# A cross network on one Trainium2 core: the state is kept as a factor c, and the last sums move to TensorE

## The chip, the cores and the metric

The kernel runs on one core of a Trainium2 chip. A core has five engines with queues of their own: TensorE (PE, matmuls; PEld is its weight load), VectorE (DVE), ScalarE (ACT), GpSimd (POOL) and SyncE (SP), which here only issues DMA. SBUF is the working memory with 128 partitions; PSUM holds what TensorE accumulates. The metric is the device time of one execution in microseconds, as the median of several runs. Before the change it is 131.3 us (three runs, 131.0 to 131.58).

## The reference

```python
B, F, D, L = 4096, 26, 16, 6          # Din = 416
x = x0
for l in range(6):
    x = x0 * (x @ ws[l] + bs[l]) + x
return x
```

All data are bf16. x0 is 4096 x 416, ws is 6 x 416 x 416. Every layer multiplies elementwise by the same x0 and adds the old x. So every x is x0 times some factor c: c starts at 1 and gains x @ ws[l] + bs[l] in each layer.

## The kernel before

The state is held transposed: the features lie on the partitions and the 4096 rows of the batch along the free axis. The 416 features are three full blocks of 128 (index m or k, tiles `XM`) and a remainder of 32. The remainders of four groups of 512 rows are packed on the 128 partitions of `XR`. The batch is cut in two halves (s = 0, 1) of 2048 rows, each of four groups (g) of 512.

Layer 0 (`first_layer`, L208) and layers 1 to 4 (the loop from L282) compute the transposed product. A tile is a pair (s, m): 48 matmuls of 512 columns (L181) and four for the remainder rows (L187) fill two PSUM tiles (`pts`, h = 0, 1) of 128 x 1024. PSUM holds four such tiles in all (pool `psum`, 4 buffers), and they are handed on in a ring. `finish` calls `ew_main` for each h: ScalarE moves the tile out of PSUM and adds the bias (L165), VectorE multiplies by x0 (L166) and adds the old state (L169). The tiles of a layer are taken in pairs: (0,0), (0,1), then the remainder of both halves (`rem_pair`), then (0,2), (1,0), then (1,1), (1,2). The input of each layer and its output alternate between `XM[1]` and `XM[2]`.

Layer 5 (from L315) is computed with the batch rows on the partitions, so that its result can be stored directly: 32 blocks of 128 rows x 416 columns, eight "quads" (`quads`) of four blocks. For each block TensorE runs three matmuls of 416 columns (L327), one for the remainder (L333) and one for the bias (L336). Then `ew` (L347): ScalarE casts out of PSUM (L354), VectorE multiplies by rows of x0 (`X0rows`, L355), adds rows of the layer-4 state (`XLrows`, L344), and the block is stored. The addition of one block is pinned behind the multiplication of the next (`pending`, `close_sum`). Nine groups are handled as pairs, the other 14 blocks singly; the final store is issued from ScalarE's queue, the others from SyncE's.

`XLrows` is the layer-4 state turned back to rows by DMA: `xl_dmat` (L204) issues one transpose of 128 x 2048 per tile (s, m) when that tile's state is ready, and `rem_pair` issues one small transpose per half into `scrR`. `xl_rem` (L276) lets ScalarE copy `scrR` into the last 32 columns of `XLrows`. It is pinned (`keep_in_program_order`): the copy for half 0 stands in ScalarE's queue in front of the four evacuations of tiles (1,1) and (1,2), the copy for half 1 behind them.

Each engine works through its own queue in order. A scheduler places the instructions of one program on the queues and adds the semaphore waits; instructions marked `keep_in_program_order` are not moved.

Of the kernel before, what the change touches and what calls it, by code (L numbers as in the profile page):

```python
# [9 lines left out]
ACT = mybir.ActivationFunctionType  # L10
ALU = mybir.AluOpType
# [5 lines left out]
def kernel(  # L17
# [7 lines left out]
    nc = tc.nc  # L25
# [23 lines left out]
    dz = const.tile([P, 2], FP32)  # L49
    warm = const.tile([P, CW], BF16)  # L50
    ones = const.tile([P, P], BF16)
    WM = const.tile([P, L, NK, D], BF16)
    WR = const.tile([P, L, D], BF16)
    WD = const.tile([P, L, NG, R], BF16)
    bsb = const.tile([L, D], BF16)
    bLr = const.tile([P, D], BF16)
    bM = const.tile([P, NK, L], FP32)
    bR = const.tile([P, L], FP32)
    X0rows = big.tile([P, NBT, D], BF16)
    XLrows = big.tile([P, NBT, D], BF16)  # L60
    scrR = [big.tile([P, 4, P], BF16, name=f"scrR{s}") for s in range(NS)]
    xrem = big.tile([P, 16, R], BF16)
    xrig = big.tile([P, NS, 4, P], BF16)
    XRd = big.tile([P, NS * CW], BF16)
    XM = [big.tile([P, NK, B], BF16, name=f"XM{i}") for i in range(3)]
    XR = [big.tile([P, NS * CW], BF16, name=f"XR{i}") for i in range(3)]

    def col0(s, g):
        return SW * s + CW * g
# [76 lines left out]
    def bias_setup():  # L146
        pb = psum.tile([P, 4, 8], BF16, tag="ps", name="pb")
        for m in range(NK):
            nc.tensor.transpose(pb[:, m, 0:L], bsb[0:L, 128 * m:128 * m + 128], ident[0:L, 0:L])
        for g in range(NG):  # L150
            nc.tensor.transpose(pb[32 * g:32 * g + 32, 3, 0:L], bsb[0:L, NK * P:D], ident[0:L, 0:L], tile_position=(0, 32 * g))  # L151
        nc.vector.tensor_copy(bM[:], pb[:, 0:NK, 0:L])  # L152
        nc.vector.tensor_copy(bR[:], pb[:, 3, 0:L])

    def x0_rem(s, tpr):
        for i in range(4):
# [2 lines left out]
            to = XR[0] if dst == src else XRd  # L159
            nc.vector.tensor_copy(to[dst, CW * s:CW * s + CW], tpr[src])  # L160

    def ew_main(l, s, m, h, pt, cur, nxt, pin=False):
        c0 = col0(s, 2 * h)
        t = tpool.tile([P, 2 * CW], BF16, name="t")
        nc.scalar.activation(t[:], pt[:].rearrange("p a b -> p (a b)"), ACT.Identity, bias=bM[:, m, l:l + 1], scale=1.0)  # L165
        prod = nc.vector.tensor_tensor(out=t[:], in0=t[:], in1=XM[0][:, m, c0:c0 + 2 * CW], op=ALU.mult)  # L166
        if pin:
            tc.keep_in_program_order(prod)
        nc.vector.tensor_tensor(out=nxt[:, m, c0:c0 + 2 * CW], in0=t[:], in1=cur[:, m, c0:c0 + 2 * CW], op=ALU.add)  # L169

    def ew_rem(l, s, pr, curR, nxtR):
        tr = tpool.tile([P, 2 * CW], BF16, name="t")
        nc.scalar.activation(tr[:, 0:CW], pr, ACT.Identity, bias=bR[:, l:l + 1], scale=1.0)  # L173
        nc.vector.tensor_tensor(out=tr[:, 0:CW], in0=tr[:, 0:CW], in1=XR[0][:, CW * s:CW * s + CW], op=ALU.mult)  # L174
        nc.vector.tensor_tensor(out=nxtR[:, CW * s:CW * s + CW], in0=tr[:, 0:CW], in1=curR[:, CW * s:CW * s + CW], op=ALU.add)  # L175

    def mm_full(l, s, m, g, pts, cur, first, last):
        c0 = col0(s, g)
        for k in range(NK):
            for q in range(4):  # L180
                nc.tensor.matmul(pts[g // 2][32 * q:32 * q + 32, g % 2, :], lhsT=WM[:, l, k, 128 * m + 32 * q:128 * m + 32 * q + 32],  # L181
                                 rhs=cur[:, k, c0:c0 + CW], start=(first and k == 0), stop=(last and k == NK - 1),
                                 tile_position=(0, 32 * q))

    def mm_row(l, s, m, pts, curR, first, last):
# [5 lines left out]
    def mm_rem(l, s, pr, cur, curR):  # L191
        for g in range(NG):
            nc.tensor.matmul(pr[32 * g:32 * g + 32, :], lhsT=WD[:, l, g, :], rhs=curR[:, CW * s:CW * s + CW],  # L193
                             start=True, stop=False, tile_position=(0, 32 * g))
        for k in range(NK):
            for g in range(NG):
                c0 = col0(s, g)
                nc.tensor.matmul(pr[32 * g:32 * g + 32, :], lhsT=WM[:, l, k, NK * P:D], rhs=cur[:, k, c0:c0 + CW],  # L198
                      start=False, stop=(k == NK - 1), tile_position=(0, 32 * g))

    def new_pts():
        return [psum.tile([P, 2, CW], FP32, tag="ps", name=f"pt{h}") for h in range(2)]

    def xl_dmat(s, k, nxt):  # L204
        nc.sync.dma_start_transpose(out=XLrows[:, 16 * s:16 * s + 16, 128 * k:128 * k + 128],
                                    in_=nxt[:, k, SW * s:SW * s + SW])

    def first_layer(s):  # L208
        cur, curR, nxt, nxtR = XM[0], XR[0], XM[1], XR[1]

        def full(pt, m, h, gl, after_row):
            c0 = col0(s, 2 * h + gl)
            for k in range(NK):
                nc.tensor.matmul(pt[:, gl, :], lhsT=WM[:, 0, k, 128 * m:128 * m + 128], rhs=cur[:, k, c0:c0 + CW],  # L214
                                 start=(k == 0 and not after_row), stop=(k == NK - 1 and after_row))

        def row(pt, m, h, opens):
# [25 lines left out]
        row(pa[2], 2, 0, False)  # L243
        row(pa[1], 1, 0, False)
        for m in range(NK):
            ew_main(0, s, m, 0, pa[m], cur, nxt)
        for m in range(NK):
            if m:
                pb.append(ph(m))
# [6 lines left out]
        if s == 0:  # L256
            x0_rem(1, pr[:, 1, :].bitcast(BF16)[:, 0:CW])
        for m in range(NK):
            ew_main(0, s, m, 1, pb[m], cur, nxt, pin=(s == 0))
        ew_rem(0, s, pr[:, 0, :], curR, nxtR)  # L260

    bias_setup()
    pe_filler(1, CW)
    for s in range(NS):
        first_layer(s)

    def rem_pair(l, cur, curR, nxtR, feeds_last):
        pr2 = psum.tile([P, 2, CW], FP32, tag="ps", name="pr2")
        for s in range(NS):
            mm_rem(l, s, pr2[:, s, :], cur, curR)  # L270
        for s in range(NS):
            ew_rem(l, s, pr2[:, s, :], curR, nxtR)
            if feeds_last:
                nc.sync.dma_start_transpose(out=scrR[s][:], in_=nxtR[:, CW * s:CW * s + CW])

    def xl_rem(s):  # L276
        tc.keep_in_program_order(
            nc.scalar.copy(XLrows[:, 16 * s:16 * s + 16, NK * P:D].rearrange("p (g i) r -> p i g r", g=NG),
                           scrR[s][:].rearrange("p i (g r) -> p i g r", g=NG)))

    cur, curR = XM[1], XR[1]
    for l in range(1, LL):  # L282
        nxt, nxtR = XM[1 + (l % 2)], XR[1 + (l % 2)]
        feeds_last = (l == LL - 1)
        tiles = [(s, m) for s in range(NS) for m in range(NK)]
        pts = {}

        def finish(t):
            s, m = t
            for h in range(2):  # L290
                ew_main(l, s, m, h, pts[t][h], cur, nxt)
            if feeds_last:
                xl_dmat(s, m, nxt)

        for n in range(0, len(tiles), 2):
            ta, tb = tiles[n], tiles[n + 1]
            pts[ta] = new_pts()
            for g in range(NG):
                mm_full(l, ta[0], ta[1], g, pts[ta], cur, True, False)
            mm_row(l, ta[0], ta[1], pts[ta], curR, False, True)  # L300
            pts[tb] = new_pts()
            mm_row(l, tb[0], tb[1], pts[tb], curR, True, False)
            if feeds_last and n == 4:
                xl_rem(0)
            finish(ta)
            for g in range(NG):
                mm_full(l, tb[0], tb[1], g, pts[tb], cur, False, True)
            finish(tb)
            if n == 0:
                rem_pair(l, cur, curR, nxtR, feeds_last)  # L310
        if feeds_last:
            xl_rem(1)
        cur, curR = nxt, nxtR
# [3 lines left out]
    NQ = len(quads)  # L317
    KD = NK * P

    def q_cols(q, g):  # L320
        s, i = quads[q]
        c = col0(s, g) + 128 * i
        return slice(c, c + 128)

    def mm_q_full(q, g, py, closes):
        for k in range(NK):
            nc.tensor.matmul(py[:, 0:D], lhsT=cur[:, k, q_cols(q, g)], rhs=WM[:, l, k, :],  # L327
                             start=((not closes) and k == 0), stop=(closes and k == NK - 1))

    def mm_q_rem(q, py, done):  # L330
# [7 lines left out]

    pending = []

    def close_sum():
        while pending:
            o, t, xl, dst, eng = pending.pop()
            tc.keep_in_program_order(nc.vector.tensor_tensor(out=o, in0=t, in1=xl, op=ALU.add))  # L344
            eng.dma_start(dst, o)

    def ew(q, g0, n, src, eng):  # L347
        s, i = quads[q]
        b0 = 16 * s + 4 * g0 + i
        b = slice(b0, b0 + 4 * (n - 1) + 1, 4)  # L350
        t = tpool.tile([P, 2 * CW], BF16, name="t")
        o = opool.tile([P, 2, D], BF16, name="o")
        tv = t[:, 0:n * D].rearrange("p (a d) -> p a d", a=n)
        nc.scalar.copy(tv, src)  # L354
        tc.keep_in_program_order(nc.vector.tensor_tensor(out=tv, in0=tv, in1=X0rows[:, b, :], op=ALU.mult))  # L355
        close_sum()
        pending.append((o[:, 0:n, :], tv, XLrows[:, b, :], out_v[:, b, :], eng))

    PAIRS = [(0, 0), (0, 1), (1, 0), (1, 1), (2, 0), (2, 1), (3, 0), (3, 1)]
    TURNS = [(0, 0), (0, 1), (1, 0), (2, 0), (3, 0), (1, 1), (2, 1), (3, 1)]  # L360
# [2 lines left out]
    for q, at, done in rounds:  # L363
# [12 lines left out]
        for u in range(done, 8):  # L376
# [2 lines left out]
                close(u, 1)  # L379
            elif u % 2:  # L380
                close(u - 1, 2)
    close_sum()


# [28 lines left out]
```

## Time and profile before

| what | value |
|---|---|
| median of three runs | 131.3 us (131.0 to 131.58) |
| profiled execution, first to last instruction (span) | 128.9 us |
| profiled execution, whole time | not recorded; span and median differ by 2.4 us |
| mean granted TensorE clock | 0.998 |
| TensorE busy | 123.1 us, 96% of the span |
| VectorE busy | 107.1 us, 83% |
| ScalarE busy | 86.9 us, 67% |
| layer 5 begins on TensorE | 103.78 us |

Times inside the span are counted from its start. A group's row gives the line, the engine, the operation, what it writes and reads, how often, its busy time and the mean time of one. A number in brackets in the timeline is the time that the engine stood idle before the row, and what released it. In SyncE's queue the duration of a row is the time that issuing took, not the time of the transfer.

### The profile page before, as it was taken

The numbers are of one execution on the slowest core, as the hardware profiler recorded it, in microseconds if no ns is written. First come the engines' busy times: TensorE is split into PE (matmuls) and PEld (weight loads), VectorE is DVE, ScalarE is ACT, GpSimd is POOL, SyncE is SP. The second block draws the span as 40 slices with busy tenths as digits, with TensorE's granted clock in tenths as the row PEclk, the third lists the DMA queues.
The fourth block names the chain that finished last, engine by engine and source line by source line (L and its number), as shares of the span: only waits on it lengthen the run. The fifth ranks groups of instructions, "written<-read, shape, count | busy, mean of one in ns | idle before, by whom it ended". The sixth has DMA issues, their size and how long they took to land.

```text
span 128.9 us, 3973 instructions
## 1 busy us (share of the span) xinstructions
PE 123.1 (96%) x1690; PEld 54.9 (43%) x1690; DVE 107.1 (83%) x197; ACT 86.9 (67%) x99; POOL 5.9 (5%) x18
## 2 busy tenths in 40 slices
PE   6999999999999999999999999999999999999960
PEld 2343443354444444444444444444444445445420
DVE  1032979999999898989898989898989899898991
ACT  0426783987848577848668848668847896569670
POOL 4022200600000000000000000000000000000000
PEclk9999999999999999999999999999999999999999
DMA  3999999999990000000000000000297999995754
GB/s 106 237 203 217 170 158 260 247 328 333 336 299 11 5 0 8 0 0 5 0 5 0 5 0 5 0 5 0 42 166 164 123 219 178 187 323 188 231 179 139
DMA packets 42102, 16.37 MB, mean 127 GB/s; under 512 B 30906, under 2 KB 42084, under 8 KB 42084
## 3 DMA queue, kind: packets, MB, share of 16 engines
q1 hardware_dynamic: 39416, 15.56, 54.6%
q10 hardware_dynamic: 2668, 0.56, 2.3%
q8 instruction: 13, 0.21, 0.7%
q14 instruction: 5, 0.04, 0.1%
HBM read 6.15 MB, written 3.41 MB: 74 GB/s over the span
## 4 chain that ended last, share of the span: by engine, by line
PE 80%; DMA 8%; DVE 5%; issue 2%; SPq 1%; ACT 1%; DVEq 0%
PE pt L181 49%; PE ph L214 9%; DMA XM<-in_x_dram 8%; PE py L327 8%; PE pt L187 5%; PE pr L198 5%; DVE t L355 3%; DVE o L344 2%; PE pr L193 2%; SPq L76 1%; PE py L333 1%; PE ph L221 1%; PE py L336 1%; ACT t L354 1%; PE pr L157 0%
## 5 line engine op out<-in xcount | busy, mean ns | idle before, releaser
L181 PE MATMUL pt<-XM,WM 128*32 128x512 bf16 x1152 | 65.2, 379 | 0.0
L165 ACT ACTIVATE t<-pt,bM 128x1024 bf16<-128x1024 f32 x48 | 49.6, 1115 | 18.3 <-PE pt L187 18.3
L166 DVE TENSOR_TENSOR t<-t,XM 128x1024 bf16<-128x1024 bf16 x60 | 41.4, 690 | 5.3 <-ACT t L165 5.3
L169 DVE TENSOR_TENSOR XM<-t,XM 128x1024 bf16<-128x1024 bf16 x60 | 41.8, 696 | 3.4
L181 PEld LDWEIGHTS <-WM 128*32 128x32 bf16 x1152 | 29.7, 97 | 33.8 <-issue 5.1
L354 ACT CAST t<-py 128x416 bf16<-128x416 f32 (+1 forms) x23 | 14.8, 642 | 4.8 <-PE py L327 2.1
L327 PE MATMUL py<-WM,XM 128*128 128x416 bf16 x96 | 17.7, 340 | 0.0
L214 PE MATMUL ph<-XM,WM 128*128 128x512 bf16 x72 | 16.5, 379 | 0.1
L165 ACT ACTIVATE t<-ph,bM 128x1024 bf16<-128x1024 f32 x12 | 12.5, 1114 | 4.4 <-PE ph L221 4.4
L327 PEld LDWEIGHTS <-XM 128*128 128x128 bf16 x96 | 9.0, 98 | 8.5 <-issue 1.4
L355 DVE TENSOR_TENSOR t<-t,X0rows 128x416 bf16<-128x416 bf16 (+1 forms) x23 | 10.4, 454 | 1.2 <-ACT t L354 1.2
L214 PEld LDWEIGHTS <-WM 128*128 128x128 bf16 x72 | 6.8, 98 | 8.6 <-issue 1.3
L344 DVE TENSOR_TENSOR o<-t,XLrows 128x416 bf16<-128x416 bf16 (+1 forms) x23 | 10.3, 451 | 0.0
L173 ACT ACTIVATE t<-pr,bR 128x512 bf16<-128x512 f32 x10 | 6.4, 684 | 2.7 <-PE pr L198 2.1
L198 PE MATMUL pr<-XM,WM 128*32 128x512 bf16 x120 | 8.2, 379 | 0.0
L187 PE MATMUL pt<-XR,WR 32*128 32x512 bf16 x96 | 7.3, 379 | 0.0
L141 PE MATMUL wps<-warm 128*128 128x512 bf16 (+1 forms) x11 | 4.4, 593 | 1.2 <-DVE warm L94 1.2
L175 DVE TENSOR_TENSOR XR<-t,XR 128x512 bf16<-128x512 bf16 x10 | 4.2, 423 | 0.7
L198 PEld LDWEIGHTS <-WM 128*32 128x32 bf16 x120 | 3.2, 97 | 3.1
L106 ACT ACT_TABLE_LOAD x1 | 1.3, 1283 | 4.3 <-DMA WM<-in_ws_dram 4.3
L174 DVE TENSOR_TENSOR t<-t,XR 128x512 bf16<-128x512 bf16 x10 | 4.2, 418 | 0.0
L152 DVE CAST bM<-pb 128x18 f32<-128x18 bf16 x1 | 0.2, 177 | 4.6 <-PE pb L151 4.6
(39 smaller groups left out, 33.6 us busy)
## 6 DMA issues: line engine op xcount, KB each, us to landing
X0rows<-in_x_dram SPq DMA_DIRECT2D x4, 832.0 KB, 11.6
out_dram<-o SPq DMA_DIRECT2D x9, 208.0 KB, 2.4
WM<-in_ws_dram SPq DMA_DIRECT2D x5, 312.0 KB
out_dram<-o SPq DMA_DIRECT2D x13, 104.0 KB, 1.7
WR<-in_ws_dram SPq DMA_DIRECT2D x4, 130.0 KB, 4.1
WM<-in_ws_dram ACTq DMA_DIRECT2D x1, 312.0 KB
XM<-in_x_dram SPq DMA_TRANSPOSE x8, 4.9
xrig<-in_x_dram ACTq DMA_DIRECT2D x4, 32.0 KB, 4.1
```

Of the source, the lines that this page charges most:

```text
L165: nc.scalar.activation(t[:], pt[:].rearrange("p a b -> p (a b)"), ACT.Identity, bias=bM[:, m, l:l + 1], scale=1.0)
L166: prod = nc.vector.tensor_tensor(out=t[:], in0=t[:], in1=XM[0][:, m, c0:c0 + 2 * CW], op=ALU.mult)
L169: nc.vector.tensor_tensor(out=nxt[:, m, c0:c0 + 2 * CW], in0=t[:], in1=cur[:, m, c0:c0 + 2 * CW], op=ALU.add)
L173: nc.scalar.activation(tr[:, 0:CW], pr, ACT.Identity, bias=bR[:, l:l + 1], scale=1.0)
L181: nc.tensor.matmul(pts[g // 2][32 * q:32 * q + 32, g % 2, :], lhsT=WM[:, l, k, 128 * m + 32 * q:128 * m + 32 * q + 32], rhs=cur[:, k, c0:c ...
L187: nc.tensor.matmul(pts[g // 2][:, g % 2, :], lhsT=WR[32 * g:32 * g + 32, l, 128 * m:128 * m + 128], rhs=curR[32 * g:32 * g + 32, CW * s:CW ...
L198: nc.tensor.matmul(pr[32 * g:32 * g + 32, :], lhsT=WM[:, l, k, NK * P:D], rhs=cur[:, k, c0:c0 + CW], start=False, stop=(k == NK - 1), tile ...
L214: nc.tensor.matmul(pt[:, gl, :], lhsT=WM[:, 0, k, 128 * m:128 * m + 128], rhs=cur[:, k, c0:c0 + CW], start=(k == 0 and not after_row), sto ...
L327: nc.tensor.matmul(py[:, 0:D], lhsT=cur[:, k, q_cols(q, g)], rhs=WM[:, l, k, :], start=((not closes) and k == 0), stop=(closes and k == NK ...
L344: tc.keep_in_program_order(nc.vector.tensor_tensor(out=o, in0=t, in1=xl, op=ALU.add))
L354: nc.scalar.copy(tv, src)
L355: tc.keep_in_program_order(nc.vector.tensor_tensor(out=tv, in0=tv, in1=X0rows[:, b, :], op=ALU.mult))
```

## The change

The kernel now keeps the factor c (`CM`, `CR`) beside x. In layer 0 ScalarE writes c directly (the bias of layer 0 has 1 added to it), and VectorE multiplies c by x0 to get x1. In layers 1 to 4 VectorE adds the layer's result into c in place and then multiplies c by x0 to get the next x. `XM[2]` and `XLrows` are gone: x after an odd layer lies in `shared`, one buffer per half, and the same buffer takes the rows of c at the end. So what the DMA turns back to rows is c of layer 4 (`cl_dmat`, `cl_dmat_rem`), and it is written over x2, the input of layer 4.

In layer 5 a block becomes (sum + c) times x0: VectorE adds the rows of c to the cast block, then multiplies by `X0rows` into the output (`close_out`). For the last three blocks of the 32 (`SUM_ON_PE = 3`) TensorE adds the rows of c itself, by a product with the identity into the same PSUM tile; two of these are then cast and multiplied, and the very last is multiplied by VectorE straight out of PSUM, without a cast.

```diff
+    CM = big.tile([P, NK, B], BF16)
+    shared = [big.tile([P, 16, D], BF16, name=f"shared{s}") for s in range(NS)]
-    XLrows = big.tile([P, NBT, D], BF16)
...
+        nc.vector.tensor_scalar_add(bM[:, :, 0:1], bM[:, :, 0:1], 1.0)
+        nc.vector.tensor_scalar_add(bR[:, 0:1], bR[:, 0:1], 1.0)
...
-        t = tpool.tile([P, 2 * CW], BF16, name="t")
-        nc.scalar.activation(t[:], pt[:].rearrange("p a b -> p (a b)"), ACT.Identity, bias=bM[:, m, l:l + 1], scale=1.0)
-        prod = nc.vector.tensor_tensor(out=t[:], in0=t[:], in1=XM[0][:, m, c0:c0 + 2 * CW], op=ALU.mult)
+        c = CM[:, m, c0:c0 + 2 * CW]
+        if l == 0:
+            nc.scalar.activation(c, pt[:].rearrange("p a b -> p (a b)"), ACT.Identity, bias=bM[:, m, 0:1], scale=1.0)
+        else:
+            t = tpool.tile([P, 2 * CW], BF16, name="t")
+            nc.scalar.activation(t[:], pt[:].rearrange("p a b -> p (a b)"), ACT.Identity, bias=bM[:, m, l:l + 1], scale=1.0)
+            nc.vector.tensor_tensor(out=c, in0=c, in1=t[:], op=ALU.add)
+        prod = nc.vector.tensor_tensor(out=nxt(m, s, 2 * h * CW, 2 * CW), in0=c, in1=XM[0][:, m, c0:c0 + 2 * CW], op=ALU.mult)
...
-        nc.vector.tensor_tensor(out=nxt[:, m, c0:c0 + 2 * CW], in0=t[:], in1=cur[:, m, c0:c0 + 2 * CW], op=ALU.add)
...
+    def cl_dmat(s, k):
+        tc.keep_in_program_order(nc.sync.dma_start_transpose(out=shared[s][:, :, 128 * k:128 * k + 128],
+                                                             in_=CM[:, k, SW * s:SW * s + SW]))
...
             finish(ta)
+            if feeds_last and n == 2:
+                cl_dmat(0, 0)
+                cl_dmat(0, 1)
+                cl_dmat_rem(0)
+                cl_dmat_rem(1)
...
             finish(tb)
+            if feeds_last and n == 2:
+                cl_dmat(0, 2)
+            if feeds_last and n == 4:
+                cl_dmat(1, 0)
+                cl_dmat(1, 1)
+                cl_dmat(1, 2)
...
+        if by_pe(q, g):
+            nc.tensor.matmul(py[:, 0:D], lhsT=ident[:], rhs=shared[s][:, 4 * g + i, :], start=False, stop=False)
...
+        if 4 * q + g0 == 4 * NQ - 1:
+            close_out()
+            tc.keep_in_program_order(nc.vector.tensor_tensor(out=o[:, 0:1, :], in0=src, in1=xr, op=ALU.mult))
+            eng.dma_start(dst, o[:, 0:1, :])
+            return
...
-        tc.keep_in_program_order(nc.vector.tensor_tensor(out=tv, in0=tv, in1=X0rows[:, b, :], op=ALU.mult))
-        close_sum()
-        pending.append((o[:, 0:n, :], tv, XLrows[:, b, :], out_v[:, b, :], eng))
+        if not by_pe(q, g0):
+            tc.keep_in_program_order(nc.vector.tensor_tensor(out=tv, in0=tv, in1=shared[s][:, r, :], op=ALU.add))
+        close_out()
+        pending.append((o[:, 0:n, :], tv, xr, dst, eng))
```

## The prediction

> **What bounds the kernel now.** I read the page first (busy shares, chain), then the chain in order of time, then the timeline around the hand-over from layer 4 to layer 5 and at the end, then SyncE's queue alone in short windows, one transpose per answer.
>
> ```profile
> span 128.9 us, 3973 instructions
> PE 123.1 (96%) x1690; PEld 54.9 (43%) x1690; DVE 107.1 (83%) x197; ACT 86.9 (67%) x99; POOL 5.9 (5%) x18
> PE 80%; DMA 8%; DVE 5%; issue 2%; SPq 1%; ACT 1%; DVEq 0%
> ```
>
> TensorE is busy 96% of the span and holds 80% of the chain. In order of time the chain is TensorE without a gap from 12.14 us to 115.78 us. So VectorE's and ScalarE's work costs nothing as long as it keeps ahead; a TensorE that must wait costs its whole wait.
>
> ```profile
> 92.00 2.76 PE L181 MATMUL pt<-XM,WM 128*32 128x512 bf16 x48
> 100.02 0.62 ACT L278 COPY XLrows<-scrR 128x512 bf16<-128x512 bf16 x1 [0.76 <-DMA scrR<-XR]
> 100.97 4.13 ACT L165 ACTIVATE t<-pt,bM 128x1024 bf16<-128x1024 f32 x4 [0.33 <-PE pt L187]
> 105.31 0.34 PE L333 MATMUL py<-WR,XR 32*128 32x416 bf16 x4
> 122.80 1.75 PE L327 MATMUL py<-WM,XM 128*128 128x416 bf16 x9
> 123.00 2.09 ACT L354 CAST t<-py 128x416 bf16<-128x416 f32 x4
> 125.39 0.37 DVE L355 TENSOR_TENSOR t<-t,X0rows 128x416 bf16<-128x416 bf16 x1
> 125.67 0.65 DVE L344 TENSOR_TENSOR o<-t,XLrows 128x416 bf16<-128x416 bf16 x2
> 126.35 0.38 ACTq L345 DMA_DIRECT2D out_dram<-o  x1
> ```
>
> These are start, duration, engine and line, from the timeline (core 0; the rows between are left out of the fence). The first is the last tile of half 0 in layer 4: its matmuls end at 94.76. The second is ScalarE's pinned copy of the remainder columns, which already waits 0.76 for the small transpose. The four activations behind it evacuate tiles (1,1) and (1,2); they end at 105.10, and TensorE takes the last freed buffer at 105.31 to 105.40. The slack is about a quarter of a microsecond. The last five rows are the tail.
>
> ```profile
> 91.63 2.03 SPq L205 DMA_TRANSPOSE XLrows<-XM  x1
> 94.35 3.07 SPq L205 DMA_TRANSPOSE XLrows<-XM  x1
> 97.52 2.53 SPq L274 DMA_TRANSPOSE scrR<-XR  x2
> 102.26 3.67 SPq L205 DMA_TRANSPOSE XLrows<-XM  x1
> scrR<-XR SPq DMA_TRANSPOSE x2, 2.5
> ```
>
> SyncE's queue: issuing one large transpose holds it 1.8 to 3.7 us, a small one 1.2 us, and a small one lands 2.5 us after its issue (last line, from the list of DMA issues): 97.52 + 2.5 = 100.02, exactly where ScalarE's copy starts.
>
> **Part 1, c in place of x (layers 0 to 4).** Layer 0 loses one of two VectorE operations per tile: 12 of 0.69 us and 2 of 0.42 us, 9.1 us. In layers 1 to 4 an add into c and a multiply replace a multiply and an add of the same shapes; x is ready after two operations as before. TensorE runs gapless over all this, so I take 0; a gain would need a TensorE gap that the chain does not show. The two additions of 1 to the biases (nearest rows: small VectorE casts of 0.18 us) fall into the 2.4 us in which VectorE waits for the remainder transposes at 8.6 us; cost 0, at most 0.36 without that cover.
>
> **Part 2, the transposes.** In the new order the rows of c go into the buffer that also holds the layer's input x2, so the first transpose of a half waits for the last matmul that reads x2 of that half. In the built program SyncE waits for exactly that matmul of tile (0,2): issue at 94.8 instead of 91.63. Behind it in SyncE's queue stand (0,1), both small transposes, (0,2), the three of half 1 and the outputs. Two large issues come before the small one. I take them as the same pair lasts before, 2.03 + 3.07, with 0.1 between issues: the small one starts at 100.1. The lower bound is 1.81 twice (the shortest large issue in the queue), giving 98.6; the upper 3.07 + 3.67, giving 101.7. I stay near the middle because the second issue of each pair was long in three pairs out of three (3.07, 3.67, 3.62). With 2.5 to landing: 102.6 (101.1 to 104.2).
>
> ScalarE's copy is pinned in front of the four activations and cannot be passed. It ends at 102.6 + 0.62 = 103.2; the four activations need 4.13 and end at 107.35 (105.85 to 108.95). TensorE needs the last of their buffers at 105.35, so it stops for **2.0 us** (0.5 to 3.6). A first short stop at 103.8, for tile (1,1)'s first buffer, lies inside this.
>
> What is late next: the (0,2) transpose, issued about 102.7, lands within 6.1 us (the median of the large ones), 108.8; VectorE ends layer 4 at 107.65 + 2.0 = 109.6, so the first addition of c is covered by 0.8. Half 1's transposes wait for TensorE at 103.9, before SyncE reaches them; at 2.7 us each (the mean of the six is near that) the last is issued at about 110.7 and lands at 116.8, against a first use at 116.69 + 2.0 = 118.7. VectorE then needs 1.0 us per pair of blocks (two operations started 0.5 apart) where TensorE needs 1.29, so a lag there is made up. Outputs start after 111.6 before; no engine waits for them until the end. Cost 0, up to 1 us if both covers fail.
>
> The rule against this step: the Trainium skill, "DMA: Bandwidth & Descriptors", section "Rules for kernel authors", says to issue a DMA early and wait for it late, so that its fixed cost hides under compute. Its loss, were the fixed cost all that is moved, would be the 3.2 us of later issue less 0.6 of slack, a stop of 2.6 us, and the sum would be +2.0 us instead of mine; the queue's rows give less, because the 0.65 us in which SyncE stands between the first two issues (93.66 to 94.35) goes.
>
> **Part 3, the end.** TensorE gains three matmuls 128x416: 96 such take 17.7 us, 0.184 each, +0.55 us; its last ends 124.55 + 0.55 = 125.10. Removed behind it: the last cast (0.51), one multiply and the additions of the last three blocks. Before, VectorE is the late one: two operations of 0.285 spacing per block, 0.57, against 0.54 of TensorE; it ends at 126.32. After, blocks 25 to 28 take two operations as before and are done by 124.3, block 29's multiply follows its cast, block 30's cast ends at 124.9 and its multiply lets the last one in at 125.2. That one reads f32 from PSUM, which no VectorE row here of this width does. Bounds: 0.37 (the bf16 multiply) and 0.69 (1024 wide); I take 0.51, ScalarE's cast of the same f32 tile. End 125.7, a gain of **0.6 us** (0.4 to 0.8). The output behind it leaves the same queue with the same landing.
>
> The Trainium skill, "VectorE: DVE Perf Modes", section "The TRN2 errata", prices a PSUM source at 120 cycles plus one per f32 element at 0.96 GHz: an estimate of 0.56 us for 416, which would make the gain 0.55.
>
> **Sum.** +2.0 − 0.6 = +1.4 us on a span of 128.9. The profiled execution's whole time is not recorded; span and median leave 2.4 us around it (2.1 to 2.7 for the runs of 131.0 to 131.58), which I keep. 131.3 + 1.4 = **132.7 us**. Ends: 131.3 + 0.5 − 0.8 = 131.0 and 131.3 + 3.6 − 0.4 = 134.5.
>
> **Rivals.**
> 1. The small transpose lands in time, and only the tail is left: faster. It decides if it lands before 105.35 − 4.13 − 0.62 = 100.6, so is issued by 98.1, with two large issues in 3.2 us. For it: some large issues take 1.8 us, and the stop of the transposes' packets that made others long need not come then. Against: no row has 1.6. Time 131.3 − 0.6 = 130.7, and 130.5 with the best tail.
> 2. A partial stop: both large issues short (1.81 to 2.03), the small one lands near 101.3; stop 0.5 to 1.2 us, net −0.1 to +0.6: 131.5. For it: with no wait between them the pair may run at the rate of the fast ones.
> 3. Half 1's rows come late too (upper issue times throughout): VectorE stands at block 16, its backlog holds ScalarE's buffers and TensorE stops a second time, about 1 us more: 133.7 to 134.5. For it: 1.9 us of cover against an issue spread of 1.9 us each. Against: the stop of TensorE moves the need later by the same amount.
> 4. TensorE's clock falls in the stop. The granted clock is 1.00 in every working window, and 0.94 in the 4.4 us after the last matmul: half speed only in the last half microsecond or so of it, hence about 3.9 us after work ended; the stop would have to be twice mine. Cost then: the cold fillers at the start ran 4.45 us, about half of it lost, +2.2 us: 134.9. The Trainium skill, "TensorE: Matmul & The Clock Gate", section "Part 1", puts the fall after one idle window of about 3.4 us; by that rule too a 2.0 us stop costs nothing more.
>
> **How the numbers follow.** Forecast (stop over 1.2 us): 0.62, its own range 132.0 to 133.6. Rival 1: 0.16; rival 2: 0.16; rivals 3 and 4: 0.06. About 0.5% (0.65 us) is what a measurement of this kernel can tell from no change: under 130.65 is faster, over 131.95 slower. Rival 1 sits on the lower bound; I count 0.15 as faster; its rest, rival 2 and the forecast's low edge are no change, 0.18; slower 0.67. The range leaves out the far upper end (0.08) and part of rival 1 (0.08): 130.65 to 133.6.
>
> **What would show it.** Right: SyncE's first transpose of half 0 at about 94.8; ScalarE's remainder copy waiting near 3 us for the small transpose; TensorE idle about 2 us near 105.4 behind ScalarE; the last matmul at about 127; then one f32 VectorE multiply of about 0.5 us straight to the output. Wrong: the copy waits under 1.3 us (rival 1), or the chain shows a stop at VectorE's first use of half 1's rows (rival 3).

## The result and the profile after

The changed kernel takes 134.62 us (median of four runs, 134.43 to 136.97) against 131.28 us: a ratio of 1.0263, 95% interval 1.0226 to 1.0299. It is slower by 2.6%. The forecast had the direction and the place, 132.7 us, but the measured time lies beyond its upper end of 133.6. Four runs at a lower mean granted clock stand in no ratio of this document: the one of 136.97 us here (0.971, the others 0.998 to 0.999) and three of the four of experiment 3 (137.83 to 138.18 us, 0.972 to 0.974).

The page of the changed kernel, answering to the three lines shown of before:

```profile
span 132.7 us, 3951 instructions
PE 124.1 (94%) x1691; PEld 55.4 (42%) x1693; DVE 98.6 (74%) x182; ACT 86.2 (65%) x98; POOL 5.0 (4%) x18
PE 80%; DMA 10%; ACT 4%; DVE 2%; issue 1%; DVEq 1%; ACTq 0%
```

The span is 3.8 us longer. (The profiled execution took 134.8 us, and the one of before is not recorded, so the two spans need not differ by just as much as the medians, 3.3 us.) VectorE's busy time falls by 8.5 us and this buys nothing. In the chain DMA grows from 8% to 10% and ScalarE from 1% to 4%: the chain now leaves TensorE once in the middle.

The waits (who waited for whom: total, times, longest) name that place:

```profile
ACT shared L300 <- DMA scrR<-CR: 5.1, 1, 5.1
PE py L361 <- ACT t L184: 2.1, 1, 2.1
PE py L367 <- ACT t L184: 1.0, 2, 0.7
```

ScalarE's pinned copy of the remainder columns waits 5.1 us for the small transpose (0.76 before). TensorE, which had no gap here before, then waits 3.1 us in three pieces for ScalarE. The timeline gives the times:

```profile
94.86 4.59 SPq L227 DMA_TRANSPOSE shared<-CM  x2
99.55 2.79 SPq L296 DMA_TRANSPOSE scrR<-CR  x2
104.36 0.62 ACT L300 COPY shared<-scrR 128x512 bf16<-128x512 bf16 x1 [5.05 <-DMA scrR<-CR]
104.89 4.12 ACT L184 ACTIVATE t<-pt,bM 128x1024 bf16<-128x1024 f32 x4
106.05 1.22 PE L361 MATMUL py<-WM,XM 128*128 128x416 bf16 x6 [2.15 <-ACT t L184]
108.06 0.35 PE L367 MATMUL py<-WR,XR 32*128 32x416 bf16 x2 [0.33 <-ACT t L184]
109.06 0.35 PE L367 MATMUL py<-WR,XR 32*128 32x416 bf16 x2 [0.66 <-ACT t L184]
...
127.72 1.36 DVE L378 TENSOR_TENSOR o<-t,X0rows 128x416 bf16<-128x416 bf16 x4
128.14 0.69 PE L361 MATMUL py<-WM,XM 128*128 128x416 bf16 x3
129.11 0.59 DVE L390 TENSOR_TENSOR o<-py,X0rows 128x416 bf16<-128x416 f32 x1
129.73 0.38 ACTq L391 DMA_DIRECT2D out_dram<-o  x1
```

The first large transpose of half 0 is issued at 94.86, behind the last matmul that reads x2; the small one, two large ones later, at 99.55. It lands 4.8 us after that. Copy and four activations follow, and TensorE takes the last buffer at 109.06, where it took it at 105.40 before. The three pieces of waiting come to 3.1 us and the delay to 3.7, because the matmuls between the pieces stand alone: two take 0.35 us at 108.06, where four took as long before.

The 3.8 us of span add up from these rows and those of before:

| piece | before | after | difference |
|---|---|---|---|
| end of the last matmul | 124.55 | 128.83 | +4.28: three more matmuls 0.55, the stop 3.73 (what is left) |
| from there to the end of the last VectorE operation | 1.77 | 0.87 | -0.90 |
| from there to the end of the span | 2.6 | 3.0 | +0.4 |

The last line has its own row. In SyncE's queue after, the store of the last block but one:

```profile
129.70 0.40 SPq L379 DMA_DIRECT2D out_dram<-o  x1
```

The four multiplies from 127.72 come out close together, but SyncE issues one store per 0.48 us (the store before this one was issued at 129.22), so the last but one is issued 0.6 us after its block is ready and lands within 0.2 us of the last one, which ScalarE's queue issues at 129.73. Before, the two were issued 0.29 apart (126.06 and 126.35).

### The profile page after: what moved, and what is told of

The parts are those of the page before. It is cut to its first block, busy times and chain, and to the rows that moved or that the text cites. A ratio compares the mean times of both kernels' runs of the same rounds, so it can differ in the third digit from the quotient of the medians.

```text
span 132.7 us, 3951 instructions
## 1 busy us (share of the span) xinstructions
PE 124.1 (94%) x1691; PEld 55.4 (42%) x1693; DVE 98.6 (74%) x182; ACT 86.2 (65%) x98; POOL 5.0 (4%) x18
## 3 DMA queue, kind: packets, MB, share of 16 engines
HBM read 6.15 MB, written 3.41 MB: 72 GB/s over the span
## 4 chain that ended last, share of the span: by engine, by line
PE 80%; DMA 10%; ACT 4%; DVE 2%; issue 1%; DVEq 1%; ACTq 0%
PE pt L204 42%; PE py L361 12%; PE ph L235 10%; PE pr L220 5%; PE pt L210 4%; ACT t L184 4%; DMA scrR<-CR 4%; DMA xrig<-in_x_dram 3%; DMA WM<-in_ws_dram 3%; PE pr L216 2%; DVE CM L185 1%; PE py L367 1%; PE ph L242 1%; DVE XM L186 1%; PE py L370 1%
## 5 line engine op out<-in xcount | busy, mean ns | idle before, releaser
L185 DVE TENSOR_TENSOR CM<-CM,t 128x1024 bf16<-128x1024 bf16 x48 | 32.9, 686 | 9.3 <-ACT t L184 9.3
L204 PE MATMUL pt<-XM,WM 128*32 128x512 bf16 x576 | 32.9, 379 | 0.0
L204 PE MATMUL pt<-shared,WM 128*32 128x512 bf16 x576 | 32.9, 379 | 0.0
L186 DVE TENSOR_TENSOR XM<-CM,XM 128x1024 bf16<-128x1024 bf16 x36 | 24.9, 696 | 8.6 <-ACT CM L181 6.7
L186 DVE TENSOR_TENSOR shared<-CM,XM 128x1024 bf16<-128x1024 bf16 x24 | 16.6, 692 | 1.3
L181 ACT ACTIVATE CM<-ph,bM 128x1024 bf16<-128x1024 f32 x12 | 12.5, 1114 | 4.1 <-PE ph L242 4.1
L397 DVE TENSOR_TENSOR t<-t,shared 128x416 bf16<-128x416 bf16 (+1 forms) x20 | 9.3, 467 | 1.1 <-ACT t L395 1.1
L378 DVE TENSOR_TENSOR o<-t,X0rows 128x416 bf16<-128x416 bf16 (+1 forms) x22 | 9.9, 456 | 0.0
L220 PE MATMUL pr<-XM,WM 128*32 128x512 bf16 x72 | 4.9, 379 | 0.0
L199 DVE TENSOR_TENSOR XR<-CR,XR 128x512 bf16<-128x512 bf16 x10 | 4.2, 423 | 0.7
## 6 DMA issues: line engine op xcount, KB each, us to landing
out_dram<-o SPq DMA_DIRECT2D x13, 104.0 KB, 1.7
```

Source lines behind the costliest of these rows:

```text
L181: nc.scalar.activation(c, pt[:].rearrange("p a b -> p (a b)"), ACT.Identity, bias=bM[:, m, 0:1], scale=1.0)
L185: nc.vector.tensor_tensor(out=c, in0=c, in1=t[:], op=ALU.add)
L186: prod = nc.vector.tensor_tensor(out=nxt(m, s, 2 * h * CW, 2 * CW), in0=c, in1=XM[0][:, m, c0:c0 + 2 * CW], op=ALU.mult)
```

## The experiments

Every experiment starts from the changed kernel unless it says otherwise. "Outside" is the time of a run less its own span, as the median over the undisturbed runs.

| run | edit | median us | ratio to before (95%) | span | outside |
|---|---|---|---|---|---|
| before | | 130.78 to 131.28 | 1 | 129.0 to 129.2 | 1.8 |
| the change | | 134.62 | 1.0263 (1.0226 to 1.0299) | 132.3 | 2.1 |
| 1 | small transposes first | 131.06 | 1.0028 (1.0014 to 1.0043) | 128.95 | 2.1 |
| 2 | ScalarE's copy late | 130.94 | 1.0027 (1.0009 to 1.0045) | 128.85 | 2.1 |
| 3 | kernel before, small transposes late | 135.61, one run | none | 133.8 | 1.8 |
| 4 | x2 of half 0 in its own buffer | 131.15 | 1.0029 (1.0013 to 1.0045) | 129.05 | 2.1 |
| 5 | 1, and no part 3 | 130.82 | 0.9995 (0.9983 to 1.0007) | 129.05 | 1.8 |
| 6 | 1, and stores spread | 130.89 | 1.0003 (0.9986 to 1.0020) | 128.8 | 2.1 |
| 7 | 6, two sums on TensorE | 131.17 | 1.0018 (1.0001 to 1.0035) | 129.05 | 2.1 |
| 8 | instruction fetch moved | 134.67 | 1.0276 (1.0249 to 1.0303) | 132.6 | 2.1 |
| 9 | 1, no direct multiply | 130.97 | 1.0000 (0.9987 to 1.0014) | 129.2 | 1.8 |
| 10 | 9, and stores spread | 130.80 | 0.9983 (0.9968 to 0.9998) | 129.0 | 1.8 |
| 11 | 1, only the last sum on TensorE | 131.41 | 1.0030 (1.0013 to 1.0047) | 129.3 | 2.1 |
| 12 | small transposes behind one large one | 131.27 | 1.0018 (1.0000 to 1.0037) | 129.15 | 2.1 |

### Is the wait for the small transpose the whole loss?

**Experiment 1: the small transposes first.**

```diff
+                cl_dmat_rem(0)
+                cl_dmat_rem(1)
                 cl_dmat(0, 0)
                 cl_dmat(0, 1)
-                cl_dmat_rem(0)
-                cl_dmat_rem(1)
```

> The changed kernel with one edit: on SyncE the two small transposes (remainder columns of c) go in front of the two large ones of half 0, not behind them. Theory A (the whole loss is ScalarE standing at its pinned copy until the small transpose of half 0 has landed): the small one is issued at about 95 and lands by 98, ScalarE's copy waits for nothing, TensorE has no gap near 105; what is left is the end: +0.55 us on TensorE, -0.9 between the last matmul and the last VectorE operation, +0.4 until the last store has landed, 0.05 in all; 131.4 us (131.0 to 131.8). Rival B (the large transposes being issued after 94.8 costs by itself, since half 0's rows are late for VectorE): VectorE waits at its first addition of rows, 132 to 133 us. Rival C (c in place, or the sums on TensorE, cost something in the other stages): stays over 133.5.

The timeline of this run:

```profile
94.47 2.52 SPq L296 DMA_TRANSPOSE scrR<-CR  x2
98.92 0.63 ACT L300 COPY shared<-scrR 128x512 bf16<-128x512 bf16 x1
100.75 4.13 ACT L184 ACTIVATE t<-pt,bM 128x1024 bf16<-128x1024 f32 x4 [1.20 <-PE pt L210]
104.73 0.36 PE L367 MATMUL py<-WR,XR 32*128 32x416 bf16 x4
105.10 0.34 PE L367 MATMUL py<-WR,XR 32*128 32x416 bf16 x4
```

The copy waits for nothing, ScalarE now waits for TensorE, and TensorE has no gap. The large transposes are issued later still than in the changed kernel, at 97.08 and 98.95 behind the small ones, yet no time is lost: rival B is out, and so is C, down to the 0.3% that remains.

**Experiment 2: the copy late.** The order of the DMAs is untouched; only ScalarE's queue changes.

```diff
-            if feeds_last and n == 4:
-                xl_rem(0)
             finish(ta)
...
         if feeds_last:
+            xl_rem(0)
             xl_rem(1)
```

> The changed kernel with one edit: ScalarE's pinned copy for half 0 stands behind the four evacuations of tiles (1,1) and (1,2), next to the copy for half 1; the order of the DMAs is as in the changed kernel, so the small transpose still lands at 102 to 104.4. Theory A: TensorE has no gap near 105, and the copy, at about 105.1, finds its transpose landed; 131.4 us (131.0 to 131.9). Rival B (late large rows): 132 to 133. Rival C: over 133.5.

In the timeline the two copies are one row, behind the four activations, and TensorE's remainder matmuls come without a gap:

```profile
100.71 4.13 ACT L184 ACTIVATE t<-pt,bM 128x1024 bf16<-128x1024 f32 x4 [1.71 <-PE pt L210]
104.71 1.15 ACT L300 COPY shared<-scrR 128x512 bf16<-128x512 bf16 x2
105.05 0.35 PE L366 MATMUL py<-WR,XR 32*128 32x416 bf16 x4
```

The small transpose of half 0 lands at 104.0 here, as late as in the changed kernel, and nobody minds. VectorE waits 0.7 us at its first rows of c, without effect. So the late landing alone costs nothing; it costs because a pinned copy that needs it stands in front of four evacuations that TensorE needs.

**Experiment 3: the same wait in the kernel before.** The small transposes go behind the large one of tile (0,2), and all are pinned in that order.

```diff
-        nc.sync.dma_start_transpose(out=XLrows[:, 16 * s:16 * s + 16, 128 * k:128 * k + 128],
-                                    in_=nxt[:, k, SW * s:SW * s + SW])
+        tc.keep_in_program_order(nc.sync.dma_start_transpose(out=XLrows[:, 16 * s:16 * s + 16, 128 * k:128 * k + 128],
+                                                             in_=nxt[:, k, SW * s:SW * s + SW]))
...
             ew_rem(l, s, pr2[:, s, :], curR, nxtR)
-            if feeds_last:
-                nc.sync.dma_start_transpose(out=scrR[s][:], in_=nxtR[:, CW * s:CW * s + CW])
...
             finish(ta)
+            if feeds_last and n == 2:
+                for s in range(NS):
+                    tc.keep_in_program_order(nc.sync.dma_start_transpose(out=scrR[s][:], in_=nxtR[:, CW * s:CW * s + CW]))
```

> The kernel before with one edit: on SyncE the two small transposes go behind the large one of tile (0,2). No other part of the change is in it. Theory A: the small one is issued at about 101.2 and lands at 103.7 or later, ScalarE's copy ends 0.6 later, its four activations 4.13 after that, at 108.5; TensorE, which would take the last buffer at 105.35, stands about 3.1 us: 134.4 us (133.8 to 135.2). Rival C (the loss belongs to other parts of the change): 131.3, as before.

The timeline, and below it the stretches of the stop and the 3.2 us behind it (the column behind the five engines is the granted clock):

```profile
100.70 3.63 SPq L306 DMA_TRANSPOSE scrR<-XR  x2
105.44 0.62 ACT L276 COPY XLrows<-scrR 128x512 bf16<-128x512 bf16 x1 [6.35 <-DMA scrR<-XR]
105.96 4.12 ACT L165 ACTIVATE t<-pt,bM 128x1024 bf16<-128x1024 f32 x4
107.12 2.24 PE L328 MATMUL py<-WM,XM 128*128 128x416 bf16 x6 [3.44 <-ACT t L165]
109.30 0.53 PE L334 MATMUL py<-WR,XR 32*128 32x416 bf16 x4
110.66 4.39 PE L328 MATMUL py<-WM,XM 128*128 128x416 bf16 x24
```

```profile
103.70:107.10 3.40, 0.00 (x0) 0.00 (x1) 0.00 (x0) 1.66 (x3) 0.00 (x0) 0.97 0.78 130
107.10:110.30 3.20, 3.18 (x18) 1.10 (x21) 3.06 (x5) 3.20 (x4) 0.00 (x0) 0.50 0.37 69
110.30:114.00 3.70, 3.70 (x27) 1.87 (x20) 3.56 (x7) 2.75 (x4) 0.00 (x0) 1.00 0.78 146
```

Without any part of the change, the late small transpose alone makes the kernel before slower than the changed one: 135.61 us in this run, over the 134.4 that was expected. The wait alone makes a loss of this size; rival C is out from this side too. The surplus is the landing once more: issued at 100.70, the small transpose lets the copy start at 105.44, 4.7 us later, where the landing was expected at 103.7 or later, 2.5 us after its issue, and all behind it shifts along. The 24 matmuls begin at 110.66, 4.90 us later than before (105.76), and the span is 4.9 us longer. Something else is new: TensorE stood still for 3.44 us, and its granted clock then fell to half for about 3.4 us. The six matmuls took 2.24 us where they take 1.23. Here this cost next to nothing, because TensorE was waiting for ScalarE's activations anyway: they end at 110.08, and the 24 matmuls begin 0.58 us behind that, against 0.51 in the changed kernel at full clock (109.01 and 109.52).

**Experiment 4: no wait for TensorE.** Half 0 of x2 gets a buffer of its own, so the rows of c are not written over it.

```diff
+    x2own = big.tile([P, NK, SW], BF16)
...
     def x2_cols(k, s, c, n):
+        if s == 0:
+            return x2own[:, k, c:c + n]
```

> The changed kernel with one edit: half 0 of x2 lies in a buffer of its own, so the rows of c of half 0 are not written over it and the first large transpose waits for VectorE alone; the order on SyncE and ScalarE is that of the changed kernel. Theory A: issue near 91, small transpose landed by 100.5, copy as in the kernel before, no gap on TensorE; 131.4 us (131.0 to 131.8). Rival (the place in the queue alone decides, not the wait for TensorE): the small one still lands after 101.5 and TensorE stands over 1 us, over 132.4.

The first transpose is issued at 91.11, the copy starts at 99.54 without a wait, and TensorE has no gap. So the queue's order, which is that of the changed kernel, is harmless as long as its first entry need not wait for the last reader of x2.

**Experiment 12: one large transpose in front.**

```diff
                 cl_dmat(0, 0)
-                cl_dmat(0, 1)
                 cl_dmat_rem(0)
                 cl_dmat_rem(1)
+                cl_dmat(0, 1)
```

> The changed kernel with one edit: on SyncE the two small transposes stand behind one large one, not two. Theory A: half 0's first large transpose is issued at 94.8, the small one at about 97, landed at 99.5; ScalarE reaches its copy at 99.3, so it waits 0.2, within the slack of about 0.6, and TensorE has no gap; ratio 1.003, as with the small ones first. Rival (the wait for TensorE alone is enough for a stop): TensorE stands over 0.5 us, ratio over 1.006.

```profile
94.81 2.01 SPq L227 DMA_TRANSPOSE shared<-CM  x1
99.79 0.62 ACT L300 COPY shared<-scrR 128x512 bf16<-128x512 bf16 x1 [0.54 <-DMA scrR<-CR]
100.96 4.13 ACT L184 ACTIVATE t<-pt,bM 128x1024 bf16<-128x1024 f32 x4 [0.55 <-PE pt L210]
```

The wait for TensorE is there (94.81), the copy waits 0.54, and the four activations still wait 0.55 for TensorE. So, as the queue stands, it takes both the late first entry and two large transposes in front of the small one to make the stop.

### Why was the stop 3.7 us and not 2.0?

ScalarE's part was right: from the start of the copy to TensorE's last freed buffer it is 4.70 us (104.36 to 109.06), and 4.75 was reckoned. The issue was even a little early, 99.55 for 100.1. What was wrong is the landing. The small transposes' issues in the changed kernel, from the instructions on that line:

```profile
DMA to landing us min/median/max: 3.7/4.3/4.8
```

Before, both took 2.5 us. The DMA engines in the window from 101 to 105 us of the changed kernel, in forty slices of 0.1 us:

```profile
DMA  9999994108000499999990000000001004999999
GB/s 218 231 228 205 212 225 100 11 0 164 0 0 0 90 218 195 218 205 192 90 19 0 5 8 10 8 10 10 10 10 16 0 8 82 169 184 241 192 205 212
q8 instruction: 1, 0.02, 2.0%
```

From about 103.1 to 104.2 next to nothing moves. (The shorter gap at 101.8 to 102.2 lies between the two small transposes; experiment 1 has one of 0.4 us there without a fetch.) One instruction fetch of 16 KB lies in the window; it starts at 101.94. A transfer reports its landing in sixteen parts: fifteen of the small transpose's came by 102.25, the sixteenth at 104.34. The same picture, a fetch and one straggler of sixteen, stands in experiment 2 (fetch at 101.59, fifteen by 101.95, the last at 104.0) and in experiment 4 for a large transpose (103.63, 104.11, 105.66).

**Experiment 8: the fetch moved.**

```diff
-    pe_filler(2, 2 * P)
-    pe_filler(8, CW)
+    pe_filler(60, 72)
```

> The changed kernel, order of DMAs and of ScalarE unchanged; only the ten matmuls that warm TensorE up at the start are replaced by sixty narrow ones of nearly the same total width, 100 more instructions in TensorE's stream. In the changed kernel a 16 KB instruction fetch starts at 101.94 and the small transpose's sixteenth landing comes at 104.34, the other fifteen by 102.25. A fetch takes 256 instructions of 64 bytes, about 7.1 us of this stage, so the one at 101.94 moves to about 99.1. Theory F (the fetch holds up one of the sixteen landings): all sixteen land within 0.3 us of each other, at 102.2 to 103.2; TensorE stands 1.6 to 2.6 us, not 3.7; ratio to the kernel before 1.014 (1.009 to 1.019). Rival (the late landing has another cause, the transposes in front of it): landing at 104 or later again, ratio 1.024 or more.

TensorE's stream runs 1.6 us later than in the changed kernel, which the new fillers were not meant to do: in the first 20 us it waits 1.6 us in four pieces for input (the first large transpose is then issued at 96.48, not 94.86). So the ratio, 1.0276, is not the 1.014 of theory F and can't decide either. Inside the span:

```profile
98.56 3.62 SPq L226 DMA_TRANSPOSE shared<-CM  x1
104.83 0.62 ACT L299 COPY shared<-scrR 128x512 bf16<-128x512 bf16 x1 [3.90 <-DMA scrR<-CR]
106.51 1.22 PE L360 MATMUL py<-WM,XM 128*128 128x416 bf16 x6 [0.99 <-ACT t L183]
109.53 0.35 PE L366 MATMUL py<-WR,XR 32*128 32x416 bf16 x2 [0.65 <-ACT t L183]
```

The fetch now starts at 100.68, where the second large transpose is being issued. The small one lands 2.5 us after its issue again, its sixteen parts within 0.2 us; but the large issue in front of it takes 3.62 instead of 2.47. From the first large issue to the landing it is 8.3 us here, 8.4 in the kernel before and 9.5 in the changed kernel; TensorE's pieces of waiting come to 2.0 us for 3.1. So the landing came as theory F had it, though not at the hour that it named. Where the fetch falls decides which transfer it holds up, and falling on the last parts of the awaited one is the dear place.

All traces agree. In three of them a fetch starts between the issue and the landing of half 0's small transpose, and it lands late: 4.8 us after its issue in the changed kernel and in experiment 2, 4.7 in experiment 3 (fetch at 102.95). In the other eleven no fetch starts there, and it takes 2.4 to 2.9 us. The kernel before and experiments 4 and 8 are among these, with two large transposes in front as in the changed kernel, so the transposes in front are not enough. No kernel here has the same timing and no fetch, so the fetch is not isolated further.

### What the end is worth

**Experiment 5: no part 3.** The last three blocks are cast, added and multiplied on VectorE like the others.

```diff
-    SUM_ON_PE = 3
+    SUM_ON_PE = 0
...
-        if 4 * q + g0 == 4 * NQ - 1:
-            close_out()
-            tc.keep_in_program_order(nc.vector.tensor_tensor(out=o[:, 0:1, :], in0=src, in1=xr, op=ALU.mult))
-            eng.dma_start(dst, o[:, 0:1, :])
-            return
```

> The changed kernel with the small transposes first, and without part 3: no sums on TensorE, the last three blocks are cast, added and multiplied on VectorE like the others. So what is left of the change is c in place of x. Theory A (c in place is neutral inside the span): span as in the kernel before, 129.0, no gap on TensorE from layer 0 to layer 5. The three kernels run so far that keep c without the stop have 2.1 us outside the span where the kernel before has 1.8; if that belongs to c, the ratio is 1.002 (1.000 to 1.004); if it belongs to the sums on TensorE or the direct multiply, it goes and the ratio is 1.000.

0.9995 (0.9983 to 1.0007): c in place of x costs and gains nothing, although VectorE is busy 8 us less (99.0 for 107.1). And the time outside the span goes back from 2.1 to 1.8 us.

**Experiments 6 and 7: the stores spread, and two sums in place of three** (both with the small transposes first).

```diff
-            ew(q + u // 4, u % 4, n, tiles[tl][:, a:a + n, 0:D], nc.scalar if q + 2 == NQ and u == 7 else nc.sync)
+            ew(q + u // 4, u % 4, n, tiles[tl][:, a:a + n, 0:D], nc.scalar if q + 2 == NQ and u == 6 else nc.sync)
...
-    SUM_ON_PE = 3
+    SUM_ON_PE = 2
```

> The changed kernel with the small transposes first, and with one more edit: the store of the last block but one is issued from ScalarE's queue and the last from SyncE's, where the changed kernel issues the last but one from SyncE (at 129.70 in its profile, 0.6 after its block was ready, since every store holds that queue for 0.48) and the last from ScalarE (129.73). Theory A (the end is held by SyncE's queue): the last landing comes 0.3 to 0.4 earlier, ratio to the kernel before 1.000 (0.998 to 1.002), against 1.003 with the small transposes first alone. Rival (the last store's own time from VectorE's end on decides): unchanged, 1.002 to 1.004.

> As the run with the spread stores, but TensorE adds c for the last two blocks, not three. TensorE saves 0.18, VectorE gains one addition (0.285) in the last row of blocks, where it ends behind TensorE. Theory A: VectorE's last multiply begins 0.1 to 0.2 earlier, since TensorE's last matmul sets it; ratio 0.998 (0.996 to 1.001). Rival (VectorE's queue sets it): 0.1 to 0.3 later, 1.001 to 1.003.

Experiment 6 gives 1.0003, 0.25% under experiment 1, as theory A had it, though the two intervals overlap. Experiment 7 gives 1.0018, which is its rival's figure and not theory A's: its interval reaches from no change to 1.0035, and it is no better than three sums.

**Experiments 9 and 11: which part brings the 0.3 us outside.** In 9 the direct multiply is taken out (the five lines removed in experiment 5) and the three sums stay; in 11 `SUM_ON_PE = 1`, and the direct multiply stays.

> The changed kernel with the small transposes first and with three sums on TensorE, but the last block too is cast by ScalarE before VectorE multiplies it. The time outside the span is 1.8 us in the kernel before and in the run without any of part 3, and 2.1 in all runs with part 3. If the direct multiply out of PSUM brings the 0.3, it is 1.8 here; if the sums on TensorE bring it, 2.1. Inside the span the last VectorE operation ends 0.3 later than with the direct multiply (cast 0.51 and multiply 0.37 for 0.59), still 0.3 earlier than in the kernel before. Ratio 0.999 (0.996 to 1.002) in the first case, 1.004 (1.002 to 1.006) in the second.

> The changed kernel with the small transposes first, with the direct multiply of the last block, whose c TensorE must then add, but with no other sum on TensorE. If the direct multiply brings the 0.3 us outside the span, it is 2.1 here; if it grows with the number of sums, about 1.9. Inside the span VectorE's queue sets the end again: 125.95 to 126.2 for its last operation against 126.32 in the kernel before. Ratio 1.002 (1.000 to 1.004).

It is the direct multiply of VectorE out of PSUM. Outside the span, run by run: 1.73 to 1.80 us without it (experiment 9, twelve runs), 2.04 to 2.14 with it (experiment 11, twelve runs). The number of sums on TensorE does not matter. Inside the span the direct multiply saves less than expected: the last VectorE operation ends 0.96 us after the last matmul in experiment 9 (126.25 and 125.29) and 0.87 in the changed kernel, not 0.3 apart. In experiment 11 it ends at 126.66, not at 125.95 to 126.2. Why one such instruction lengthens what lies outside the profiled span, no run here tells.

**Experiment 10: the best of these.** Experiment 9 with the stores of experiment 6.

> As the run without the direct multiply, with the store of the last block but one issued from ScalarE and the last from SyncE. If SyncE's queue holds the end, 0.1 to 0.3 us less than that run: ratio 0.997 (0.994 to 1.000). Rival: no difference.

0.9983 (0.9968 to 0.9998): 0.2% under the kernel before, at the edge of what can be told apart. Its last operations:

```profile
124.33 1.36 DVE L378 TENSOR_TENSOR o<-t,X0rows 128x416 bf16<-128x416 bf16 x4
125.48 0.51 ACT L390 CAST t<-py 128x416 bf16<-128x416 f32 x1 [0.20 <-PE py L361]
125.72 0.37 ACTq L379 DMA_DIRECT2D out_dram<-o  x1
126.02 0.38 DVE L378 TENSOR_TENSOR o<-t,X0rows 128x416 bf16<-128x416 bf16 x1 [0.33 <-ACT t L390]
```

VectorE is no longer late: it waits for the last cast and is done 0.4 us behind it. The third row is the store of the last block but one; the last store leaves from SyncE's queue.

## Why the prediction was right and wrong

**Part 1** was right: worth nothing (experiment 5).

**Part 2, the mechanism**, was right in each link: the first large transpose behind the last read of x2 (94.8 predicted, 94.86 measured), two large issues, the small one (100.1; 99.55), the copy, the four activations, TensorE without a buffer. Experiments 1, 2, 4 and 12 each remove one link and the stop is gone; what stays, 0.2 to 0.3%, goes with part 3 (experiment 5). Experiment 3 puts the stop into the kernel before.

**Part 2, the size**, was wrong in one term: "With 2.5 to landing". It was 4.8 us, and 2.1 of the 2.3 too many are the wait for the last of its sixteen parts. I took the one duration that the trace of before shows for this transfer and gave it no range, while I gave the issues a range for the very same stalls (the long ones of 3.07 to 3.67). The copy started at 104.36; the range had 101.1 to 104.2. Of the 3.73 us of stop, 2.0 were predicted and 2.3 more come from the landing, less 0.55 for the earlier issue.

The rule weighed there, the Trainium skill, "DMA: Bandwidth & Descriptors", "Rules for kernel authors" (issue early, wait late), gave a stop of 2.6 us; the trace has 3.7, more than either sum. (The rows of before give 0.69 us for the 0.65 between the first two issues, which changes nothing.)

**Part 2, what is late next**, was right: half 0's and half 1's rows arrived in time.

**Part 3** was wrong: a gain of 0.6 us was predicted; the difference of experiments 1 and 5 is a loss of 0.3% (1.0028 to 0.9995), 0.4 us. Three terms: VectorE's last operation ended 0.35 us earlier relative to the stop, not 0.6, because the direct multiply waited for the multiply before it to end (129.08) and took 0.59 (in experiment 11 too it begins at 126.07, 0.02 behind the one before it, with TensorE done since 125.01); the stores gave back 0.4, because "the output behind it leaves the same queue with the same landing" left SyncE's queue out, which could not keep up with four blocks in a row (spreading the stores gave 0.25% in experiment 6 and 0.17% in experiment 10, with intervals that overlap); and 0.33 were added outside the span, which "I keep" had fixed. (The 2.4 us kept there set one run's span against the median of others; run by run it is 1.8 before and 2.1 after.) The Trainium skill, "VectorE: DVE Perf Modes", "The TRN2 errata", gave an estimate of 0.56 us for the direct multiply; the measured 0.59 is nearer to that than my 0.51.

**The rivals.** Rivals 1, 2 and 3 did not come. Rival 4, the falling clock, was dismissed with "the stop would have to be twice mine". The profiled run kept its clock through 3.1 us of waiting in three pieces, but experiment 3 lost it within 3.44 us in one piece, and then for about 3.4 us. The Trainium skill, "TensorE: Matmul & The Clock Gate", "Part 1", says that one idle window of about 3.4 us puts the clock to half. The traces agree in the length, but the window need not be idle throughout, and the 3.9 us that I read from the end of the trace is no bound. In experiment 9 TensorE's last matmul ends at 125.29, and the granted clock (the column behind the five engines) falls 2.2 us later:

```profile
124.07:127.48 3.41, 1.22 (x7) 0.49 (x5) 1.80 (x6) 1.37 (x3) 0.00 (x0) 1.00 0.62 204
127.48:129.05 1.57, 0.00 (x0) 0.00 (x0) 0.00 (x0) 0.00 (x0) 0.00 (x0) 0.50 0.16 51
```

The 3.41 us before the fall hold 1.22 us of matmuls. The emptiest 3.41 us of the changed kernel's profile (102.65 to 106.06) hold 1.3, so its stop lies close to this edge. Whether it fell over it in a run without a profile stays open. The price put on this rival, 2.2 us, did not show in experiment 3's profile, where TensorE was waiting for ScalarE.

## What to carry to other kernels

When a transfer is made later, follow what is pinned behind its arrival, not only who reads its data: here 0.6 us of ScalarE's work, which VectorE needed only at 111.48, 6.5 us after it was done, stood in front of four evacuations that TensorE needed at once, and moving either of the two mended it. Give a transfer's landing a range as wide as the issues around it show, all the more where it crosses other traffic such as instruction fetches. An engine that is relieved at the very end hands its blocks over faster; look at the queue that stores them before counting the gain.

## What was not expected of the hardware

- After every 16 KB instruction fetch that met these transposes, in all fourteen traces, the DMA engines moved next to nothing (under 25 GB/s) for 1.1 to 1.4 us, 1.9 in experiments 2 and 4; where this hit the end of a transfer (the changed kernel, experiments 2 and 4), one of the sixteen parts of its landing came 1.6 to 2.1 us behind the other fifteen (102.25 and 104.34 in the changed kernel, 101.95 and 104.0 in experiment 2).
- One VectorE multiply of 128x416 f32 out of PSUM at the end went with 0.33 us more outside the profiled span in every kernel that had it (2.1 us in the changed kernel and in experiments 1, 2, 4, 6, 7, 8, 11 and 12) and in none that had not (1.8 us before and in experiments 3, 5, 9 and 10).
- TensorE's granted clock changed only at whole multiples of 3.413 us from its first change, in every trace (experiment 3: at 4.51, 106.91, 110.32 and 134.21). It fell to 0.50 where the 3.41 us before held 1.2 us of matmuls or less (1.22 in experiment 9, 0.97 in experiment 1, 0.18 in experiment 3) and stayed where they held 1.7 or more (1.71 in experiment 6, 2.03 in the changed kernel's stop). So how long a stop it bears depends on where the stop falls between two such times.
